# A two-layer matmul kernel on one core: which PSUM banks its products take, and in which order

## The chip, the core and the metric

The kernel runs on one core of a Trainium2 chip. The time is device microseconds of one execution: three runs of the kernel before took 566.67, 566.69 and 568.35 us, the median is 566.69. The profiled execution is a fourth.

The engines are named as in the profile: PE (TensorE, the matmuls), DVE (VectorE), ACT (ScalarE), POOL (GpSimd), SP (SyncE, which issues most loads). Results of PE land in PSUM, which has eight banks; a bank holds 128 x 512 fp32 numbers, one product group. Everything else lies in SBUF.

## The reference

A decayed linear attention over 16 heads (2 batches of 8) of 768 positions and 64 features gives 1536 tokens of 512 features. Two layers follow, each 512 to 2048 to 512, the first with ELU between, the second with a leaky rectifier whose slope is a given number per feature:

```python
x = attention(q, k, v, lam)               # 1536 x 512, causal, decay lam per head
h = x @ w_in;   g = where(h > 0, h, exp(minimum(h, 0)) - 1);       x = g @ w_out
h = x @ w2_in;  g = maximum(h, 0) + alpha * minimum(h, 0);         y = g @ w2_out
```

All is fp32.

## The kernel before

**Precision.** Each fp32 operand is split into a high and a low part in fp32r, and a product is three matmuls: high by high, high by low, low by high. The names end in `h` and `l` (`x0h`, `x0l`, `wah`, `wal`, `wdh`, `wdl`, `wsh`, `wsl`, `qb1h`, ...). The low part of anything is a subtraction by `sub` (L347), which may run on DVE or POOL; the high part is a copy or cast by `copy` (L339, L341) on ACT or DVE. The weights come in by DMA (`raw`), and ACT (L373) and DVE (L375, L378, L381) turn their bits into `wt` before the split.

**Attention** (to about 46 us): twelve blocks of 128 tokens, each with scores (L487), the decay mask on DVE (L492), the state (L531) and the outputs (L556, L562). `run_up` (L474) are matmuls of a constant tile ahead of the first block: three before `lam` is spread (L630), six behind.

**The layers.** The tokens are three chunks of 512: t = 0, 1, 2. Each layer has NU = 8 steps j of 256 hidden features. The way *up* of chunk 0 is `plain` (L707 on): two products of four times three matmuls of 128 x 512, in two groups of six, the result in one bank. Chunks 1 and 2 share one scheme (`seven`, L744 on): seven products of six matmuls instead of eight, on sums of weights (`ws`) and of tokens (`qT1`, `qT2`, `qT3`). Its banks are 0, 1 and 2, turned by j. Four of its results in a bank are not yet final when a product ends: `kept` copies a bank to a `step` tile, and `tile` adds a bank and such a copy (L766). In step j = 0 all three chunks go by `plain`.

`finish` (L670) takes a finished sum to `g`: relu on ACT (L675 from PSUM, L680 from SBUF), in layer 0 exp (L686), a combine on DVE (L688 in layer 0, L692 in layer 1), and the split into high and low of a slot `g`. The way *down* (`down`, L785) is one group of six matmuls (L802) for each t and quarter e, in banks 5, 6 and 7, added to `acc` on DVE (L813).

**Order.** PE's order is written out by hand: `merge(up, dn, lead)` gives out `lead` groups of `up`, then one `up` and one `down` in turn. For the other engines a planner (`Plan`) takes operations by due time as engines come free by its own costs; an operation marked shared (both inputs in SBUF) isn't begun while one of the other of DVE and POOL runs. Each engine then runs its list in that order.

Before step j of `seven`, `weights`, `sums` and `weights_down` convert what the next step needs. `combine` makes the sums of tokens between the layers and behind the attention.

Of the kernel before, what the change touches and what calls it, by code (L numbers as in the profile page):

```python
# [12 lines left out]
ALU = mybir.AluOpType  # L13
# [12 lines left out]
NU = NF // 2  # L26
# [186 lines left out]
def attention_two_layers(  # L213
# [57 lines left out]
    def ut(i):  # L271
        return step(i)
# [341 lines left out]
    def begin():  # L614
# [15 lines left out]
        pe(0.3, lambda: nc.tensor.matmul(  # L630
            out=p_[:, 0:H], lhsT=row[:, 0:128], rhs=row[:, 128:128 + H], start=True, stop=True),
           [b_row, b_one], [b_ps[k]])
        run_up(6)
        op({"DVE": 0.17}, lambda e: nc.vector.tensor_copy(lam_sb, p_[:, 0:H]),
           [b_ps[k]], [b_lam])

# [30 lines left out]
    gslot = {}  # L667
# [39 lines left out]
    def plain(l, j, t=0):  # L707
        for q in range(2):
            f = 2 * j + q
            k = 3 + turn("up", 2)  # L710
            s = j % 2
            mms = [(w, x, cc) for w, x in ((0, 0), (0, 1), (1, 0)) for cc in range(NCC)]
            xs = both[t] if t else x0
            if t:
                b_x = [b_quad[f"B{c}{t}", p, o] for p in range(2) for c in (1, 2)
                       for o in range(2)]
            else:
                b_x = [b_x0[p, o] for p in range(2) for o in range(4)]

            for g in range(2):  # L720
                def run(g=g, q=q, k=k, xs=xs):
                    for i in range(6 * g, 6 * g + 6):
                        w, x, cc = mms[i]
                        nc.tensor.matmul(  # L724
                            out=banks[k], lhsT=wa[s][w][:, cc, q * 128:(q + 1) * 128],
                            rhs=xs[x][:, cc, :], start=i == 0, stop=i == 11)
                yield pe(6 * MM, run, b_x + b_wa[s], [b_ps[k]])
            finish(l, f, lambda k=k: banks[k], b_ps[k], (l, j, q, t), True)
# [15 lines left out]
    def seven(l, j):  # L744
        s = j % 2
        for n, (a, b, k, opens, closes) in enumerate(PRODUCTS):
            k = (k + j) % 3

            def run(a=a, b=b, k=k, opens=opens, closes=closes):
                i = 0  # L750
                for w, x in ((0, 0), (0, 1), (1, 0)):
                    for cc in range(2):
                        nc.tensor.matmul(  # L753
                            out=banks[k], lhsT=left(s, a, w)[:, cc, :],
                            rhs=quad(b, x)[:, cc, :], start=bool(opens and i == 0),
                            stop=bool(closes and i == 5), skip_group_check=True)
                        i += 1
            reads = [b_quad[b, p, o] for p in range(2) for o in range(2)]
            reads += b_wa[s] if a[0] == "A" else b_ws
            yield pe(6 * MM, run, reads, [b_ps[k]])  # L760

            def kept(u, k=k):
                copy(lambda: ut(u), lambda: banks[k], [b_ps[k]], [b_ut[u]], 512, True)

            def tile(u, q, t, k=k):
                op({"DVE": vec(512)}, lambda e: nc.vector.tensor_tensor(  # L766
                    out=ut(u), in0=banks[k], in1=ut(u), op=ALU.add),
                   [b_ps[k], b_ut[u]], [b_ut[u]])
                finish(l, 2 * j + q, lambda: ut(u), b_ut[u], (l, j, q, t), False)
            if b == "B11":  # L770
                kept(0)
            elif b == "B21":
                tile(0, 0, 1)
            elif b == "T1":
                kept(1)
            elif b == "T2":
                kept(2)
            elif b == "B22":
                tile(2, 0, 2)
            elif b == "T3":  # L780
                tile(1, 1, 2)
            else:
                finish(l, 2 * j + 1, lambda k=k: banks[k], b_ps[k], (l, j, 1, 1), True)

# [60 lines left out]

    def downs(l, j, ts):
        for t, e in ts:
            yield from down(l, j, t, e, 2 if (l, j, t, e) == (1, NU - 1, 1, 3) else 1)
            if e == 3:
                gfree.extend(gslot[l, j, q, t] for q in range(2))  # L850

    T0 = [(0, e) for e in range(4)]
    T12 = [(t, e) for t in (2, 1) for e in range(4)]
# [2 lines left out]
    def build():  # L856
# [46 lines left out]
        for l in range(2):  # L903
            if l == 0:
                merge(chain(plain(0, 0, 1), plain(0, 0, 0), at_once(second), plain(0, 1),
                            plain(0, 0, 2)), downs(0, 0, T0), 10)
            else:
                merge((), downs(1, 0, T0))
                merge(chain(plain(1, 0, 1), plain(1, 0, 2)), downs(1, 1, T0))
# [3 lines left out]
            for j in range(1, NU - 1):  # L913
                merge(chain(seven(l, j), at_once(weights, l, j + 1), at_once(sums, l, j + 1),
                            plain(l, j + 1)),
                      chain(downs(0, 1, T0) if (l, j) == (0, 1) else (), downs(l, j - 1, T12),
                            at_once(weights_down, l, j + 1),
                            downs(l, j, T0) if j > 1 else ()), 2 * (l == 1 and j == 1))
            j = NU - 1
            merge(seven(l, j), chain(downs(l, j, T0), downs(l, j - 1, T12)))  # L920
            if l == 1:
                merge((), downs(1, j, T12))
                continue
# [71 lines left out]
```

## Time and profile before

| what | value |
|---|---|
| median of three runs | 566.69 us |
| profiled execution | 567.25 us, its span 565.5 us |
| PE busy | 554.6 us (98%) |
| DVE, ACT, POOL busy | 412.8, 293.6, 306.8 us |
| granted clock, mean of the span | 0.997 |

A row of an engine in time gives its start, how long it lasted, the work, how many instructions, and in brackets the idle time before it and what ended it. Rows of PE hold several matmuls; a matmul starts 0.227 us behind the one before it when nothing waits, and lasts longer than that since they overlap. PEclk is the clock that the throttle granted, as a share of full speed.

### The profile page before, as it was taken

Reading aid. Unit: us, or ns where it says so; the run is one execution under the profiler, and the core shown is the slowest. Engines: PE = TensorE matmul, PEld = TensorE weight load, DVE = VectorE, ACT = ScalarE, POOL = GpSimd, SP = SyncE. Lnnn points to the kernel's source line nnn. Section 1 sums busy time; section 2 is a strip of 40 time slices with the busy share of each in tenths; the row PEclk is TensorE's granted clock in tenths of the full one; section 3 lists DMA queues with packets and bytes.
Section 4 is the critical chain, followed back from the end, with each engine's and each line's share of the span. In section 5 each row is a group of like instructions: output and inputs, shape, how many; then the busy total and the mean of one; then the engine's idle time right before and its main releaser. Section 6 shows DMA issues by size and latency. Waiting matters only on the chain.

```text
span 565.5 us, 7443 instructions
## 1 busy us (share of the span) xinstructions
PE 554.6 (98%) x2870; PEld 458.7 (81%) x2870; DVE 412.8 (73%) x532; ACT 293.6 (52%) x462; POOL 306.8 (54%) x207
## 2 busy tenths in 40 slices
PE   9998999999999999999999989999999999999997
PEld 8887878888888888888878868888888888888886
DVE  6898888647576674768984988667877787877464
ACT  2575676856364646455655626746453434434220
POOL 4885534475746647555648843675746473742000
PEclk9999999999999999999999989999999999999999
DMA  8962422031304021222221202041322222000104
GB/s 346 403 259 81 145 74 75 21 129 32 119 0 150 0 77 72 74 76 75 75 84 65 75 1 69 6 149 37 114 75 74 75 74 75 0 2 0 56 20 148
DMA packets 18309, 49.24 MB, mean 87 GB/s; under 512 B 1250, under 2 KB 1506, under 8 KB 18274
## 3 DMA queue, kind: packets, MB, share of 16 engines
q1 hardware_dynamic: 18128, 48.25, 24.4%
q8 instruction: 22, 0.36, 0.3%
q10 hardware_dynamic: 146, 0.52, 0.2%
q14 instruction: 13, 0.11, 0.1%
HBM read 45.62 MB, written 3.15 MB: 86 GB/s over the span
## 4 chain that ended last, share of the span: by engine, by line
PE 81%; DVE 10%; DMA 3%; issue 2%; ACT 2%; SPq 0%; ACTq 0%; DVEq 0%
PE ps L802 41%; PE ps L753 22%; PE ps L724 15%; DVE wt L381 2%; DMA raw<-in_w1o 1%; DVE wt L378 1%; DVE g L347 1%; DMA raw<-in_w1i 1%; DVE wt L375 1%; DVE acc L813 1%; PE ps L487 1%; DMA raw<-in_w2o 1%; PE ps L474 1%; DVE step L688 1%; PE ps L556 1%
## 5 line engine op out<-in xcount | busy, mean ns | idle before, releaser
L813 DVE TENSOR_TENSOR acc<-ps,acc 128x512 f32<-128x512 f32 (+1 forms) x169 | 115.7, 686 | 93.5 <-PE ps L802 92.5
L347 POOL TENSOR_TENSOR g<-step,g 128x512 fp32r<-128x512 f32 x66 | 103.9, 1576 | 92.7 <-ACT g L339 92.6
L802 PE MATMUL ps<-wdh,g 128*128 128x512 f32 (+1 forms) x388 | 119.2, 388 | 1.9 <-DVE g L347 1.9
L802 PE MATMUL ps<-g,wdh 128*128 128x512 f32 x384 | 118.5, 390 | 0.0
L802 PEld LDWEIGHTS ps<-wdh,g 128*128 128x128 f32 x388 | 73.0, 189 | 17.3 <-DVE g L347 2.3
L802 PEld LDWEIGHTS ps<-g,wdh 128*128 128x128 f32 x384 | 72.0, 188 | 15.5 <-DVE g L347 0.3
L339 ACT CAST g<-step 128x512 fp32r<-128x512 f32 x96 | 59.3, 620 | 43.2 <-DVE step L692 29.0
L802 PE MATMUL ps<-g,wdl 128*128 128x512 f32 x192 | 74.8, 390 | 1.1 <-DVE wdl L347 1.1
L802 PE MATMUL ps<-wdl,g 128*128 128x512 f32 (+1 forms) x194 | 75.2, 387 | 0.0
L347 POOL TENSOR_TENSOR wsl<-wt,wsh 128x1024 fp32r<-128x1024 f32 x13 | 33.7, 2590 | 48.7 <-PE ps L802 19.1
L675 ACT ACTIVATE step<-ps 128x512 f32<-128x512 f32 x54 | 32.4, 599 | 41.8 <-PE ps L724 33.7
L680 ACT ACTIVATE step<-step 128x512 f32<-128x512 f32 x42 | 26.5, 632 | 48.6 <-DVE step L766 48.2
L378 DVE SCALAR_TENSOR_TENSOR wt<-raw,wt 128x1024 uint32<-128x1024 uint32 x32 | 49.6, 1556 | 0.2
L347 POOL TENSOR_TENSOR wt<-wt 128x256 f32<-128x256 f32 x50 | 41.2, 841 | 13.0 <-DVE wt L381 12.2
L347 POOL TENSOR_TENSOR wal<-wt,wah 128x1024 fp32r<-128x1024 f32 x12 | 28.9, 2405 | 33.1 <-ACT wah L339 33.1
L339 ACT COPY step<-ps 128x512 f32<-128x512 f32 x42 | 24.7, 589 | 36.4 <-PE ps L753 36.2
L381 DVE SCALAR_TENSOR_TENSOR wt<-raw,wt 128x1024 uint32<-128x1024 uint32 x32 | 43.5, 1363 | 0.0
L802 PEld LDWEIGHTS ps<-g,wdl 128*128 128x128 f32 x192 | 36.0, 188 | 8.9 <-DVE wdl L347 1.5
L802 PEld LDWEIGHTS ps<-wdl,g 128*128 128x128 f32 x194 | 36.6, 189 | 7.5
L373 ACT ACTIVATE wt<-raw 128x1024 f32<-128x1024 f32 x32 | 36.4, 1139 | 7.6 <-DMA raw<-in_w1i 2.5
L766 DVE TENSOR_TENSOR step<-ps,step 128x512 f32<-128x512 f32 x42 | 28.9, 688 | 14.1 <-PE ps L753 14.0
L724 PE MATMUL ps<-x0l,wah 128*128 128x512 f32 x128 | 38.9, 389 | 0.0
(129 smaller groups left out, 1004.5 us busy)
## 6 DMA issues: line engine op xcount, KB each, us to landing
raw<-in_w1i SPq DMA_DIRECT2D x8, 1024.0 KB, 5.5
raw<-in_w1o SPq DMA_DIRECT2D x8, 1024.0 KB, 4.8
raw<-in_w2i SPq DMA_DIRECT2D x8, 1024.0 KB, 5.4
raw<-in_w2o SPq DMA_DIRECT2D x8, 1024.0 KB, 4.9
blk<-in_kqT SPq DMA_DIRECT2D x12, 512.0 KB, 6.9
blk<-in_vk SPq DMA_DIRECT2D x9, 512.0 KB, 6.9
out<-acc SPq DMA_DIRECT2D x11, 256.0 KB, 2.0
blk<-in_vk ACTq DMA_DIRECT2D x1, 512.0 KB, 6.0
```

The lines of the kernel that those rows point to most:

```text
L339: nc.scalar.copy(dst(), src())
L347: lambda e: on(e).tensor_tensor(out=dst(), in0=a(), in1=b(), op=alu),
L373: op({"ACT": 1.14}, lambda e: nc.scalar.mul(t, upper.bitcast(F32), 2.0 ** -112), [b_r], [b_t])
L378: op({"DVE": vec(1024)}, lambda e: nc.vector.scalar_tensor_tensor(out=tu, in0=lower, scalar=29, in1=tu, op0=ALU.logical_shift_right, op1=A ...
L381: op({"DVE": vec(1024)}, lambda e: nc.vector.scalar_tensor_tensor(out=tu, in0=upper, scalar=0x80000000, in1=tu, op0=ALU.bitwise_and, op1=A ...
L675: op({"ACT": act(512, True)}, lambda e: nc.scalar.activation(rt(i), h(), AF.Relu, scale=-1.0), [b_h], [b_r])
L680: nc.scalar.activation(rt(i), h(), AF.Relu, scale=-1.0)
L724: nc.tensor.matmul(out=banks[k], lhsT=wa[s][w][:, cc, q * 128:(q + 1) * 128], rhs=xs[x][:, cc, :], start=i == 0, stop=i == 11)
L753: nc.tensor.matmul(out=banks[k], lhsT=left(s, a, w)[:, cc, :], rhs=quad(b, x)[:, cc, :], start=bool(opens and i == 0), stop=bool(closes an ...
L766: op({"DVE": vec(512)}, lambda e: nc.vector.tensor_tensor(out=ut(u), in0=banks[k], in1=ut(u), op=ALU.add), [b_ps[k], b_ut[u]], [b_ut[u]])
L802: nc.tensor.matmul(out=p_, lhsT=lhs, rhs=rhs, start=i == 0, stop=i == 5)
L813: op({"DVE": vec(w)}, lambda _, a=a, p_=p_: nc.vector.tensor_tensor(out=a(), in0=p_, in1=a(), op=ALU.add), [b_ps[k], *b_a], b_a)
```

## The change

Four places.

- The second `run_up` has three matmuls instead of six.
- In steps j = 0 and 1 of a layer `plain` takes the banks 3, 4, 0, 1, 2 in turn, instead of 3 and 4. From j = 2 on it takes 3 and 4 as before.
- The sums of `tile` are written to a bank of PSUM instead of the `step` tile: to the product's own bank, for T3 to bank (1 + j) % 3. `finish` reads them there: its relu is L675 instead of L680, and its combine has one operand in PSUM and isn't marked shared.
- Leads: 12 instead of 10 at the start of layer 0; 4 instead of 2 at (layer 1, j = 1); 2 instead of 0 at the last `seven` of each layer. `gfree`, the list of free slots of `g`, gets its slots back one step earlier in the construction.

```diff
-        run_up(6)
+        run_up(3)
...
-            k = 3 + turn("up", 2)
+            k = (3 + turn(("first", l), 5)) % 5 if j < 2 else 3 + turn("up", 2)
...
-            def tile(u, q, t, k=k):
+            def tile(u, q, t, k=k, to=None):
+                to = k if to is None else to
                 op({"DVE": vec(512)}, lambda e: nc.vector.tensor_tensor(
-                    out=ut(u), in0=banks[k], in1=ut(u), op=ALU.add),
-                   [b_ps[k], b_ut[u]], [b_ut[u]])
-                finish(l, 2 * j + q, lambda: ut(u), b_ut[u], (l, j, q, t), False)
+                    out=banks[to], in0=banks[k], in1=ut(u), op=ALU.add),
+                   [b_ps[k], b_ut[u]], [b_ps[to]])
+                finish(l, 2 * j + q, lambda: banks[to], b_ps[to], (l, j, q, t), True)
...
-                tile(1, 1, 2)
+                tile(1, 1, 2, to=(1 + j) % 3)
...
-            yield from down(l, j, t, e, 2 if (l, j, t, e) == (1, NU - 1, 1, 3) else 1)
-            if e == 3:
-                gfree.extend(gslot[l, j, q, t] for q in range(2))
+            parts = 2 if (l, j, t, e) == (1, NU - 1, 1, 3) else 1
+            for c, x in enumerate(down(l, j, t, e, parts)):
+                if e == 3 and c == parts - 1:
+                    gfree.extend(gslot[l, j, q, t] for q in range(2))
+                yield x
...
-                            plain(0, 0, 2)), downs(0, 0, T0), 10)
+                            plain(0, 0, 2)), downs(0, 0, T0), 12)
...
-                            downs(l, j, T0) if j > 1 else ()), 2 * (l == 1 and j == 1))
+                            downs(l, j, T0) if j > 1 else ()), 4 * (l == 1 and j == 1))
...
-            merge(seven(l, j), chain(downs(l, j, T0), downs(l, j - 1, T12)))
+            merge(seven(l, j), chain(downs(l, j, T0), downs(l, j - 1, T12)), 2)
```

Since the planner works with the new needs, its lists move too. The names in the pieces that follow: `g_689` and the like are slots of `g` (numbered anew in each kernel), `wt<-wt` is a sum of weights for `ws`, `wal`, `wdl` and `wsl` are low parts of weights.

DVE behind the attention, before. The last L575, which writes `x0l`, the input of chunk 0's products, stands right ahead of the first row; the `g` of the last row is the one that the first down group reads second:

```order
L381 SCALAR_TENSOR_TENSOR wt<-raw,wt 128x1024
L378 SCALAR_TENSOR_TENSOR wt<-raw,wt 128x1024
L688 SCALAR_TENSOR_TENSOR step<-step,ps 128x512
L347 TENSOR_TENSOR wal<-wt,wah 128x1024
L688 SCALAR_TENSOR_TENSOR step<-step,ps 128x512
L381 SCALAR_TENSOR_TENSOR wt<-raw,wt 128x1024
L347 TENSOR_TENSOR g_689<-step,g_689 128x512
L688 SCALAR_TENSOR_TENSOR step<-step,ps 128x512
L347 TENSOR_TENSOR wdl<-wt,wdh 128x1024
L688 SCALAR_TENSOR_TENSOR step<-step,ps 128x512
L347 TENSOR_TENSOR wt<-wt 128x256
L347 TENSOR_TENSOR g_733<-step,g_733 128x512
```

And now, from the same L381 to the `g` that the first down group reads second:

```order
L381 SCALAR_TENSOR_TENSOR wt<-raw,wt 128x1024
L688 SCALAR_TENSOR_TENSOR step<-step,ps 128x512
L378 SCALAR_TENSOR_TENSOR wt<-raw,wt 128x1024
L347 TENSOR_TENSOR wal<-wt,wah 128x1024
L347 TENSOR_TENSOR g_673<-step,g_673 128x512
L381 SCALAR_TENSOR_TENSOR wt<-raw,wt 128x1024
L688 SCALAR_TENSOR_TENSOR step<-step,ps 128x512 x2
L347 TENSOR_TENSOR g_717<-step,g_717 128x512
L688 SCALAR_TENSOR_TENSOR step<-step,ps 128x512
L347 TENSOR_TENSOR g_706<-step,g_706 128x512
L347 TENSOR_TENSOR wt<-wt 128x256
L347 TENSOR_TENSOR g_737<-step,g_737 128x512
```

The first L688 stands ahead of an L378 instead of behind it, `wdl` has left DVE's list here, and two slots of `g` (`g_717`, `g_706`) stand in it where `wdl` stood and after.

DVE at the last two sums of a round in layer 0 (step j = 4), before. The second L766 is the sum of T3, on which the last product waits:

```order
L813 TENSOR_TENSOR acc_72<-ps,acc_72 128x512
L766 TENSOR_TENSOR step<-ps,step 128x512
L813 TENSOR_TENSOR acc_71<-ps,acc_71 128x512
L375 TENSOR_SCALAR wt<-wt 128x1024
L766 TENSOR_TENSOR step<-ps,step 128x512
L688 SCALAR_TENSOR_TENSOR step<-step 128x512
```

And now:

```order
L814 TENSOR_TENSOR acc_72<-ps,acc_72 128x512
L375 TENSOR_SCALAR wt<-wt 128x1024
L378 SCALAR_TENSOR_TENSOR wt<-raw,wt 128x1024
L814 TENSOR_TENSOR acc_72<-ps,acc_72 128x512
L381 SCALAR_TENSOR_TENSOR wt<-raw,wt 128x1024
L767 TENSOR_TENSOR ps<-ps,step 128x512
L814 TENSOR_TENSOR acc_71<-ps,acc_71 128x512
L767 TENSOR_TENSOR ps<-ps,step 128x512
L688 SCALAR_TENSOR_TENSOR step<-step,ps 128x512
```

The conversion L375 that stood between the two sums now stands ahead of both, and so do L378 and L381.

DVE in layer 1, at the weights of step j = 1, before. The `g` at the end is read by a down group:

```order
L381 SCALAR_TENSOR_TENSOR wt<-raw,wt 128x1024
L813 TENSOR_TENSOR acc_71<-ps,acc_71 128x512
L692 SCALAR_TENSOR_TENSOR step<-step,beta,ps 128x512
L347 TENSOR_TENSOR wdl<-wt,wdh 128x1024
L347 TENSOR_TENSOR qb1l<-acc_71,qb1h 128x512
L347 TENSOR_TENSOR g_803<-step,g_803 128x512
```

And now:

```order
L381 SCALAR_TENSOR_TENSOR wt<-raw,wt 128x1024
L814 TENSOR_TENSOR acc_71<-ps,acc_71 128x512
L692 SCALAR_TENSOR_TENSOR step<-step,beta,ps 128x512
L814 TENSOR_TENSOR acc_72<-ps,acc_72 128x512
L347 TENSOR_TENSOR qb1l<-acc_71,qb1h 128x512
L692 SCALAR_TENSOR_TENSOR step<-step,beta,ps 128x512
L814 TENSOR_TENSOR acc_71<-ps,acc_71 128x512
L347 TENSOR_TENSOR wdl<-wt,wdh 128x1024
L347 TENSOR_TENSOR qb1l<-acc_71,qb1h 128x512
L347 TENSOR_TENSOR g_782<-step,g_782 128x512
```

L381, the end of the conversion, and `wdl`, `qb1l` and `g` keep their order; between L381 and `wdl` there are now three L814 (the renumbered L813), one `qb1l` and two L692.

## Rows read from the trace of the kernel before

**Rows 1.** Waits of PE: for what, us in total, times, longest

```profile
PE ps L724 <- DVE step L688: 2.1, 1, 2.1
PE ps L802 <- DVE g L347: 1.9, 1, 1.9
PE ps L802 <- DVE wdl L347: 1.1, 1, 1.1
```

**Rows 2.** PE in time, 50 to 332: start, us, work, idle before

```profile
52.57 1.07 PE L724 MATMUL ps<-qb1l,wah 128*128 128x512 f32 x4
53.48 1.07 PE L724 MATMUL ps<-qb1h,wal 128*128 128x512 f32 x4
56.68 1.20 PE L724 MATMUL ps<-x0h,wah 128*128 128x512 f32 x4 [2.13 <-DVE step L688]
...
82.03 0.50 PE L802 MATMUL ps<-g,wdl 128*128 128x512 f32 x1 [1.05 <-DVE wdl L347]
...
190.80 0.73 PE L753 MATMUL ps<-qb2h,wah 128*128 128x512 f32 x2
...
192.29 0.61 PE L802 MATMUL ps<-g,wdh 128*128 128x512 f32 x2
...
286.12 0.73 PE L753 MATMUL ps<-qb2h,wah 128*128 128x512 f32 x2 [0.65 <-DVE step L766]
...
327.35 0.50 PE L802 MATMUL ps<-wdh,g 128*128 128x512 f32 x1 [1.93 <-DVE g L347]
```

**Rows 3.** Windows: stretch, length, busy us by engine, PEclk, DMA share

```profile
2.00:36.00 34.00, 33.09 (x464) 29.25 (x463) 29.08 (x56) 17.00 (x40) 23.76 (x21) 1.00 1.02 400
...
328.00:332.00 4.00, 4.00 (x12) 3.14 (x11) 3.97 (x4) 1.31 (x2) 1.53 (x1) 0.57 0.00 0
```

**Rows 4.** PE in time, in the attention part

```profile
3.15 2.93 PE L474 MATMUL ps<-warm 128*128 128x128 f32 x12
6.01 2.60 PE L487 MATMUL ps<-blk 64*128 64x128 f32 x32
...
44.78 1.09 PE L556 MATMUL ps<-smqp,blk 128*64 128x128 f32 x16
```

**Rows 5.** Tile blk, loads issued before 1.3 us, and their landing

```profile
L331 SPq DMA_DIRECT2D blk<-in_kqT x2: 381/400/419, 0.7 to 1.2; - x2
...
DMA to landing us min/median/max: 3.3/5.4/6.0
```

**Rows 6.** DVE in time, eight places of the span

```profile
7.75 1.29 DVE L492 TENSOR_TENSOR smqp<-ps,dmst 128x512 f32<-128x512 f32 x2 [1.58 <-PE ps L487]
...
43.98 0.69 DVE L492 TENSOR_TENSOR smqp<-ps,dmst 128x512 f32<-128x512 f32 x1
...
55.95 0.68 DVE L688 SCALAR_TENSOR_TENSOR step<-step,ps 128x512 f32<-128x512 f32 x1
...
59.92 1.78 DVE L347 TENSOR_TENSOR g<-step,g 128x512 fp32r<-128x512 f32 x1
...
77.29 0.68 DVE L347 TENSOR_TENSOR g<-step,g 128x512 fp32r<-128x512 f32 x1
...
189.45 0.69 DVE L375 TENSOR_SCALAR wt<-wt 128x1024 uint32<-128x1024 uint32 x1 [0.49 <-ACT wt L373]
190.06 0.68 DVE L766 TENSOR_TENSOR step<-ps,step 128x512 f32<-128x512 f32 x1
...
324.45 2.85 DVE L347 TENSOR_TENSOR g<-step,g 128x512 fp32r<-128x512 f32 x1
```

**Rows 7.** ACT in time, ahead of the last attention blocks

```profile
36.74 1.18 ACT L373 ACTIVATE wt<-raw 128x1024 f32<-128x1024 f32 x1 [2.39 <-DMA raw<-in_w1o]
```

**Rows 8.** Groups by form, DVE: busy us, mean ns, idle before

```profile
L688 DVE SCALAR_TENSOR_TENSOR step<-step,ps 128x512 f32<-128x512 f32 x27 | 18.3, 679 | 4.1 <-ACT step L686 4.0
...
L688 DVE SCALAR_TENSOR_TENSOR step<-step 128x512 f32<-128x512 f32 x21 | 15.2, 724 | 2.0 <-ACT step L686 1.9
```

**Rows 9.** POOL in time, at E

```profile
320.59 3.39 POOL L347 TENSOR_TENSOR wsl<-wt,wsh 128x1024 fp32r<-128x1024 f32 x1
```


## The prediction

> **What bounds the kernel now.** I read PE's waits first [rows 1]: one of 2.1 us for DVE's L688, one of 1.9 for a `g`, one of 1.1 for a `wdl`. With 0.65 for an L766 [rows 2] they are 5.8 us of a span of 565.5, and beside them only short waits stand in the list: PE computes nearly all the time. No edit takes a large product away, so the change can only move these waits and what follows them. All of them are waits for DVE. The second view is PE in order of time [rows 2], which gives the waits their places: B (56.68), C (82.03), D (286.12), E (327.35). The third is the granted clock: 0.57 as the mean of the four us behind E [rows 3], so that part of it runs at the lower level, 1.2 GHz instead of 2.4. The work lost is 4 × 0.43 = 1.7 us, and E costs 1.9 + 1.7 = 3.6 us. Behind B, a longer wait, PE's next four matmuls take 1.20 us, near the 1.07 of undisturbed ones: full speed.
>
> **Start: three run-ups fewer.** A run-up is two rows of the trace, and 12 rows take 2.93 us [rows 4]: three save 1.47, if the input of the scores (L487) is there. The first load is issued at 0.7 and lands 3.3 later, at 4.0 [rows 5]; the scores could start at 4.6 instead of 6.01. L492 on DVE waits 1.58 for them at 7.75 [rows 6], so up to 1.4 us could be passed on. But at 36.74 ACT waits 2.39 us for the load of w1o [rows 7], which a faster PE can't bring sooner: the DMA engines' share is 1.02 from 2 to 36 us [rows 3], full. Behind it stands DVE's L492 of 43.98, which ends at 44.67 [rows 6]; PE's L556, which reads it, starts at 44.78 [rows 4] and shows no wait. PE arrives there just in time now, and would wait for what it had saved. I take 0; the ends are −1.4, and +0.3 (if the scores' own input is late after all).
>
> **B: five banks.** PE's third plain product waits 2.13 us [rows 2] because bank 3 is read by DVE's L688 only at 55.95 [rows 6], behind weight conversions. With five banks the third and fourth products take banks that nobody holds; their last input (L575) stands three operations ahead of that L688 on DVE, so it is there. The restart costs 1.20 − 1.07 = 0.13, and 0.2 more for the matmul in flight when PE stopped. B is worth −2.4.
>
> **What is late next: the first down group.** By the new lead PE meets it two groups later in its list, and 2.4 us earlier at each place. A group is six matmuls of (53.48 − 52.57) / 4 = 0.227 us [rows 2], so 1.36; the two add 2.7, and the group starts at the same time as before, about 66.6. It needs the second `g` 0.7 later. DVE makes that `g`; in its list three conversions, four L688, a `wal` and four other `g` or slices stand ahead. An operation of DVE with two inputs in SBUF that meets one of POOL takes longer: a `g` of 1.78 at 59.92, of 0.68 at 77.29 [rows 6]. Laying out the new order with such meetings, the `g` comes at 68.0 to 68.8, a new wait of 0.7 to 1.5; without meetings there is none; with one more there are 2.2. I take +1.0.
>
> **C.** The wait for `wdl` is 1.05 [rows 2], with its restart 1.3. On DVE `wsl`, L381 and `qT2l` stand ahead of `wdl` in the new order, as `wsl` and L381 did; I get its end at 80.3 to 80.8, where PE wants it at 79.0 to 79.5. The wait stays: 0, ends −1.3 and +1.3. B, first down and C: −1.4 together; ends −3.7 (no wait left) and +1.1.
>
> **Sums kept in PSUM.** 42 sums are written to PSUM, and 42 relus and 42 combines read it. No row shows a sum written to PSUM. The nearest is L688, which takes 679 ns with a PSUM operand and 724 without [rows 8]: −0.045 an operation. Beside PE, which waits for neither engine in this stretch but for T4 (below), I cost it at 0; without that cover it is 42 × 0.045 = −1.9, and as much on the other side. A bank is now held until the combine: sum, relu, exp, combine, four operations of some 0.68 = 2.7 us behind the product. The next product into it comes two groups later, with downs between them 4 us. In layer 1 five leading groups have no down between them, 2.7 us: the tightest place, at most +0.5.
>
> T4, the last product of a round, waits for T3's sum. From 190.80 to the next group it takes 1.49 instead of 1.36 [rows 2], and so in five rounds of layer 0. Here the sum of 190.06 started behind an L375 that had itself waited 0.49 for ACT [rows 6]. In the new order a conversion still stands right ahead of it in two of the five rounds: 3 × 0.13 = −0.4, ends 0 and −0.7.
>
> **D.** The last round of layer 0 waits 0.65 for the same sum [rows 2], behind an `x0l` on DVE. All four `x0l` are now POOL's, and lead 2 puts more downs behind the products. −0.5 in all with the restart, ends −0.8 and +0.5.
>
> **E.** DVE's `g` takes 2.85 us at 324.45 [rows 6], since it meets POOL's `wsl` (320.59, 3.39) and its neighbours [rows 9]. In the new order `wdl`, `qb1l`, `g` follow one another on DVE as before, POOL's list keeps `acc`, `wsl`, `qT1l` there, and `wdl` can't start before PE's last read of the old weights and ACT's cast behind it, which the change doesn't move. With meetings the `g` comes at 327.1 to 327.7, where PE wants it at 325.3. I take 0; ends −3.6 (no wait) and +1.3 (one more meeting).
>
> The Trainium skill speaks to both ends of E. "SBUF — State Buffer", Who interferes with whom, says that the engine which issues first holds the shared port and the other blocks for the whole instruction, so issue order decides. The meetings in rows 6 and 9 agree that both suffer; by that rule a `wdl` issued just ahead of POOL's `acc` would come out alone, E would fall to a wait of 0.9, and the total to that of rival 1. "TensorE: Matmul & The Clock Gate", What's actually happening, says that the activity window runs free of the kernel's start; by it, half clock behind a wait is a matter of when it falls. The trace agrees as far as it goes (none behind 2.13 us, some behind 1.93), and a moved E could lose its 1.7 us or a new wait gain them.
>
> **Sum.** Start 0, B, first down and C −1.4, PSUM 0, T4 −0.4, D −0.5, E 0: −2.3, and with the small gain in DVE's operations −2.4. The profiled execution took 567.25 (span 565.5 and 1.75 around it), so 564.85; the median of the runs, 566.69, is 0.56 under it: 564.3.
>
> **Rivals.**
> 1. E shortens too, its half clock included or not. For it: all is shifted by a microsecond there, and the conversions of w2o stand earlier on DVE. Against: the gate of `wdl` stands. A further −1.7 to −3.6: 560.7 to 562.6.
> 2. B's gain is given back whole at the first down (wait 2.2), D and T4 gain half: −0.2 −0.4 = −0.6, so 566.1. For it: what DVE has to do ahead of that `g` is as much in both orders. It holds, too, if the sums in PSUM do nothing at all.
> 3. Slower: the wait at the first down is long enough to be followed by half clock as at E. PE loses 2.2 + 1.7 there, and `wdl` at C, with `qT2l` ahead of it, 1.3 more: −2.4 + 5.2 = +2.8, 569.5. It decides if the second `g` is later than about 69.2, a wait like E's. Against: one wait of three above 1 us was followed by it.
> 4. All goes: −2.4 − 1.3 (C) − 1.4 (start) − 0.5 − 0.8 − 3.6 = −10.0, and no new wait: 556.7. That needs no meeting of DVE and POOL anywhere; the rows speak against.
>
> **Chances.** The forecast (562.8 to 565.6 by itself) 0.47, rival 1 0.18, rival 2 0.19, rival 3 0.10, rival 4 0.06. A measurement of this kernel can tell 0.3%, 1.7 us, from no change: faster is under 565.0, slower over 568.4. Faster: 0.40 of the forecast and rivals 1 and 4, 0.64. Same: 0.07 of the forecast, rival 2 and 0.01 of rival 3, 0.27. Slower: 0.09. The range leaves out rivals 3 and 4 and the far end of nothing else: 560.2 to 567.4.
>
> **What would show it.** In the changed kernel the third plain product should follow the second without a wait; a wait of about 1 us for a DVE `g` should stand at the first down group and one for `wdl` at 79 to 80; T4 should take 1.36 in rounds 4 to 6; a wait of about 2 us for `g` should stand near 322 to 325; and PE should wait before 45 us for what it saved at 5. No wait at the first down makes B worth its 2.4 in full; a wait of a seven product for L688 or L692 would show the PSUM term wrong; no wait for `g` in layer 1 would show E's.

## The result, and the profile after

Four runs of the changed kernel took 561.05 to 561.54 us, median 561.32; the kernel before, beside them, 566.85. The ratio is 0.9896, 95% interval [0.9879, 0.9914]: 5.5 us faster, where 2.4 were forecast. The sign was right, the time lies inside the range, the size was missed by more than a factor of two.

Where the time went is read from PE's list, which holds the same work in nearly the same order in both kernels. Each line compares the start of one instruction at the same point of it:

| up to | before | after | gained in the stretch | forecast |
|---|---|---|---|---|
| first weight product (L724) | 48.83 | 48.83 | 0 | 0 |
| second product of the first round of seven | 83.06 | 80.84 | 2.22 | 1.4 |
| first product of the last round, layer 0 | 268.75 | 265.82 | 0.71 | 0.4 |
| first down group (L802) of layer 1 | 317.56 | 313.42 | 1.21 | 0.5 |
| second plain product behind E | 332.27 | 326.25 | 1.88 | 0 |
| first product of round 2, layer 1 | 369.00 | 363.13 | -0.15 | 0 |
| last matmul | 562.07 | 556.20 | 0 | 0 |

PE of the changed kernel in order of time (start, duration, work, idle before), the places of [rows 2, 4]:

```profile
4.73 3.49 PE L487 MATMUL ps<-blk 64*128 64x128 f32 x32
8.76 0.69 PE L531 MATMUL ps<-blk,kdqs 128*64 128x64 f32 x16 [0.54 <-POOL kdqs L504]
...
44.78 1.09 PE L556 MATMUL ps<-smqp,blk 128*64 128x128 f32 x16
...
54.38 1.07 PE L724 MATMUL ps<-x0h,wah 128*128 128x512 f32 x4
...
68.23 0.50 PE L803 MATMUL ps<-g,wdh 128*128 128x512 f32 x1 [0.54 <-DVE g L347]
...
79.80 0.50 PE L803 MATMUL ps<-g,wdl 128*128 128x512 f32 x1 [0.53 <-DVE wdl L347]
...
80.84 0.62 PE L753 MATMUL ps<-qb1h,wah 128*128 128x512 f32 x2
...
188.30 0.62 PE L753 MATMUL ps<-qb2h,wah 128*128 128x512 f32 x2
...
189.66 0.62 PE L803 MATMUL ps<-g,wdh 128*128 128x512 f32 x2
...
322.94 0.50 PE L803 MATMUL ps<-wdh,g 128*128 128x512 f32 x1 [1.65 <-DVE g L347]
...
326.25 1.07 PE L724 MATMUL ps<-qb1h,wah 128*128 128x512 f32 x4
```

Of the kernel before, the rows that stand against 8.76, 80.84 and 326.25:

```profile
8.54 0.69 PE L531 MATMUL ps<-blk,kdqs 128*64 128x64 f32 x16
...
83.06 0.63 PE L753 MATMUL ps<-qb1h,wah 128*128 128x512 f32 x2
...
332.27 1.08 PE L724 MATMUL ps<-qb1h,wah 128*128 128x512 f32 x4
```

The scores start 1.28 us earlier, and L556 of [rows 4] starts at 44.78 again: the run-ups are given back. That is done by 8.76, where PE, with a first block of scores of 3.49 instead of 2.60 and a wait of 0.54 for POOL's `kdqs`, is 0.22 later than before. The third plain product follows at 54.38 without a wait. A wait of 0.54 stands at the first down group and one of 0.53 for `wdl`. T4 takes 189.66 - 188.30 = 1.36. D's wait is gone. E is still there, 1.65 for 1.93. The windows behind it (stretch, length, busy time of PE, PEld, DVE, ACT, POOL, granted clock, DMA share, GB/s) answer to [rows 3]:

```profile
324.00:328.00 4.00, 4.00 (x19) 3.33 (x18) 2.89 (x4) 2.85 (x4) 2.33 (x1) 1.00 0.00 0
328.00:332.00 4.00, 4.00 (x19) 3.30 (x19) 3.73 (x5) 0.84 (x2) 0.10 (x1) 1.00 0.02 4
```

The clock stays at 1.00 where it was 0.57, the mean of a stretch most of which was at half clock (0.50, 1.2 GHz instead of 2.4). That is the one stretch with a gain of 1.9 where the forecast had none. DVE and POOL at E, after:

```profile
314.84 2.46 DVE L347 TENSOR_TENSOR wdl<-wt,wdh 128x1024 fp32r<-128x1024 f32 x1 [0.53 <-ACT wdh L339]
317.23 2.88 DVE L347 TENSOR_TENSOR qb1l<-acc,qb1h 128x512 fp32r<-128x512 f32 x1
320.03 2.86 DVE L347 TENSOR_TENSOR g<-step,g 128x512 fp32r<-128x512 f32 x1
```

```profile
316.19 3.37 POOL L347 TENSOR_TENSOR wsl<-wt,wsh 128x1024 fp32r<-128x1024 f32 x1
319.52 2.82 POOL L347 TENSOR_TENSOR qT1l<-acc,qT1h 128x1024 fp32r<-128x1024 f32 x1
```

As in [rows 6, 9], `g` takes four times its 0.68 us. Groups by form on DVE (busy, mean ns, idle before), for [rows 8]:

```profile
L688 DVE SCALAR_TENSOR_TENSOR step<-step,ps 128x512 f32<-128x512 f32 x48 | 32.6, 681 | 4.1 <-ACT step L686 3.6
L767 DVE TENSOR_TENSOR ps<-ps,step 128x512 f32<-128x512 f32 x42 | 29.3, 698 | 19.0 <-PE ps L753 18.0 <-ACT x0h L339 0.7
```

The sums of the kernel before:

```profile
L766 DVE TENSOR_TENSOR step<-ps,step 128x512 f32<-128x512 f32 x42 | 28.9, 688 | 14.1 <-PE ps L753 14.0
```

A sum written to PSUM takes 698 ns, 10 more than one written to SBUF took.

Executions of one and the same kernel come at levels about 1.6 us apart, and each level has its own mean clock. The kernel before, 63 executions on the four chips of the experiments:

| mean granted clock | executions | time, median |
|---|---|---|
| 1.000 | 16 | 565.3 |
| 0.996 to 0.997 | 27 | 567.0 |
| 0.993 to 0.994 | 20 | 568.5 |

The profiled execution (567.25, 0.997) is of the middle level. The four runs of the changed kernel are all at 0.999 or 1.000. Level against level the change is worth 565.3 - 561.3 = 4.0 us; the other 1.5 is half clock that the kernel before has in most executions and the changed one in none. On each of the four chips the kernel before has its first level between 565.1 and 565.5 (medians), so versions that ran on different chips compare to about 0.4 us.

### The profile page after: what moved, and what is told of

Same layout as the page of the kernel before. It is cut to its first block, busy times and chain, and to the rows that moved or that the text cites. A ratio compares the mean times of both kernels' runs of the same rounds, so it can differ in the third digit from the quotient of the medians.

```text
span 559.6 us, 7427 instructions
## 1 busy us (share of the span) xinstructions
PE 551.4 (99%) x2864; PEld 457.4 (82%) x2864; DVE 397.6 (71%) x523; ACT 292.4 (52%) x461; POOL 312.6 (56%) x217
## 4 chain that ended last, share of the span: by engine, by line
PE 86%; DVE 6%; DMA 4%; ACT 2%; issue 1%; SPq 0%; ACTq 0%; DVEq 0%
PE ps L803 44%; PE ps L753 24%; PE ps L724 15%; DMA raw<-in_w1i 2%; DMA raw<-in_w1o 2%; DVE g L347 1%; PE ps L487 1%; DVE wt L381 1%; DVE wt L347 1%; PE ps L556 1%; DVE wdl L347 1%; DVE smqp L492 1%; PE ps L562 1%; PE ps L474 1%; DVE qb1l L347 1%
## 5 line engine op out<-in xcount | busy, mean ns | idle before, releaser
L814 DVE TENSOR_TENSOR acc<-ps,acc 128x512 f32<-128x512 f32 (+1 forms) x169 | 116.0, 687 | 97.4 <-PE ps L803 96.7
L347 POOL TENSOR_TENSOR g<-step,g 128x512 fp32r<-128x512 f32 x73 | 106.4, 1462 | 80.9 <-ACT g L339 80.7
L675 ACT ACTIVATE step<-ps 128x512 f32<-128x512 f32 x96 | 57.4, 598 | 95.2 <-DVE ps L767 51.4
L347 POOL TENSOR_TENSOR wsl<-wt,wsh 128x1024 fp32r<-128x1024 f32 x12 | 31.8, 2650 | 54.7 <-ACT wsh L339 33.5
L692 DVE SCALAR_TENSOR_TENSOR step<-step,beta,ps 128x512 f32<-128x512 f32 x48 | 35.7, 743 | 18.5 <-ACT step L675 18.5
L347 POOL TENSOR_TENSOR wal<-wt,wah 128x1024 fp32r<-128x1024 f32 x14 | 34.5, 2465 | 23.4 <-ACT wah L339 23.3
L381 DVE SCALAR_TENSOR_TENSOR wt<-raw,wt 128x1024 uint32<-128x1024 uint32 x32 | 44.4, 1389 | 0.0
L347 POOL TENSOR_TENSOR wdl<-wt,wdh 128x1024 fp32r<-128x1024 f32 x12 | 32.2, 2683 | 20.1 <-ACT wdh L339 19.9
L767 DVE TENSOR_TENSOR ps<-ps,step 128x512 f32<-128x512 f32 x42 | 29.3, 698 | 19.0 <-PE ps L753 18.0
L378 DVE SCALAR_TENSOR_TENSOR wt<-raw,wt 128x1024 uint32<-128x1024 uint32 x32 | 41.7, 1308 | 0.1
L347 POOL TENSOR_TENSOR wt<-wt 128x256 f32<-128x256 f32 x51 | 38.7, 774 | 5.0 <-DVE wt L381 3.9
```

Source lines behind the costliest of these rows:

```text
L347: lambda e: on(e).tensor_tensor(out=dst(), in0=a(), in1=b(), op=alu),
L378: op({"DVE": vec(1024)}, lambda e: nc.vector.scalar_tensor_tensor(out=tu, in0=lower, scalar=29, in1=tu, op0=ALU.logical_shift_right, op1=A ...
L381: op({"DVE": vec(1024)}, lambda e: nc.vector.scalar_tensor_tensor(out=tu, in0=upper, scalar=0x80000000, in1=tu, op0=ALU.bitwise_and, op1=A ...
L675: op({"ACT": act(512, True)}, lambda e: nc.scalar.activation(rt(i), h(), AF.Relu, scale=-1.0), [b_h], [b_r])
L692: op({"DVE": vec(512) + 0.06}, lambda e: nc.vector.scalar_tensor_tensor(out=rt(i), in0=rt(i), scalar=beta[:, f:f + 1], in1=h(), op0=ALU.mu ...
L767: op({"DVE": vec(512)}, lambda e: nc.vector.tensor_tensor(out=banks[to], in0=banks[k], in1=ut(u), op=ALU.add), [b_ps[k], b_ut[u]], [b_ps[to]])
```

## The experiments

**Undoing one part of the change at a time.** The run-ups:

```diff
-        run_up(3)
+        run_up(6)
```

> The changed kernel with all six run-ups again. My theory: PE waits for the same load (w1o) and DVE's L492 by 45 us in any case, so the first weight product (L724) starts at 48.83 as in both kernels, and the time is that of the changed kernel, 561.3, within 0.4. Rival (the run-ups saved are passed on): 561.3 + 1.4 = 562.7.

Measured: 561.25 (561.21 to 561.44), the time of the changed kernel. The run-ups are worth nothing either way, as forecast. The reason given, that PE waits for the load of w1o and for DVE by 45 us, is not what the rows show: the difference is gone at 8.76 us already, where L531 starts in both.

Banks 3 and 4 only:

```diff
-            k = (3 + turn(("first", l), 5)) % 5 if j < 2 else 3 + turn("up", 2)
+            k = 3 + turn("up", 2)
```

> The changed kernel, but plain products take banks 3 and 4 throughout, as before. My theory: the wait at 54.5 for L688 of 1 to 2.3 us returns, and the first down group then comes late enough to have its second g in time (0.7 returned), so the stretch to the first seven-product round loses 1.5 to 2: 562.8 to 563.3, and the rest of the trace is as in the changed kernel, without half clock. Rival A (DVE's list moves so that L688 comes at 55.0): the wait is under 0.7, time 561.3 to 561.8. Rival B (everything behind it shifts, and half clock at the wait for g in layer 1 returns): 564.5 to 565.

Measured: 563.04 (562.93 to 563.26), 1.7 more. PE, in order of time:

```profile
54.99 1.20 PE L724 MATMUL ps<-x0h,wah 128*128 128x512 f32 x4 [0.65 <-DVE step L688]
...
61.80 1.21 PE L724 MATMUL ps<-x0h,wah 128*128 128x512 f32 x4 [0.89 <-DVE step L688]
...
68.11 1.20 PE L724 MATMUL ps<-qb2h,wah 128*128 128x512 f32 x4 [0.53 <-DVE step L688]
```

One wait of 2.1 has become three of 0.5 to 0.9, for the same L688, and no half clock follows any. The theory holds in the time and in the sum of the waits, not in their form: it had one wait.

Sums in SBUF (`tile` and its T3 call as before):

```diff
-                    out=banks[to], in0=banks[k], in1=ut(u), op=ALU.add),
-                   [b_ps[k], b_ut[u]], [b_ps[to]])
-                finish(l, 2 * j + q, lambda: banks[to], b_ps[to], (l, j, q, t), True)
+                    out=ut(u), in0=banks[k], in1=ut(u), op=ALU.add),
+                   [b_ps[k], b_ut[u]], [b_ut[u]])
+                finish(l, 2 * j + q, lambda: ut(u), b_ut[u], (l, j, q, t), False)
```

> The changed kernel, but the tile sums go to SBUF and finish reads them there, as before. My theory: the product behind the T3 sum takes 1.50 again in five or six rounds of layer 0 (+0.7), the last round of layer 0 gets part of its 1.2 back, and nothing else moves: 562.0 to 563.0. Rival A (the leads alone made these gains): 561.3. Rival B (the planner's list moves so that the wait for g in layer 1 is followed by half clock): 1.7 more, 563.7 to 564.7.

Measured: 561.00 (560.83 to 561.04). The theory is wrong, and rival A is nearer by its time: T4 still takes 1.36 in all rounds of layer 0. With banks and leads, the sums in PSUM have nothing left to do.

Old leads (10, 2, 0):

```diff
-                            plain(0, 0, 2)), downs(0, 0, T0), 12)
+                            plain(0, 0, 2)), downs(0, 0, T0), 10)
...
-                            downs(l, j, T0) if j > 1 else ()), 4 * (l == 1 and j == 1))
+                            downs(l, j, T0) if j > 1 else ()), 2 * (l == 1 and j == 1))
...
-            merge(seven(l, j), chain(downs(l, j, T0), downs(l, j - 1, T12)), 2)
+            merge(seven(l, j), chain(downs(l, j, T0), downs(l, j - 1, T12)))
```

> The changed kernel with the leads 10, 2 and 0 of before. My theory: five banks take away the wait at 54.5 in any case, but the first down group comes two groups earlier and waits 2 to 3 us longer for its second g, so B's 2.3 is given back there; the last round of layer 0 loses the 0.5 to 0.8 of its T4: 563.3 to 564.5. Rival (the leads matter for nothing): 561.3, with the wait for g at the first down group below 0.6.

Measured: 563.58, at levels: 561.9 and 562.2 (clock 1.000), 563.5 to 563.8 (0.996 to 0.997), 564.8 (0.993).

```profile
68.15 0.50 PE L803 MATMUL ps<-g,wdh 128*128 128x512 f32 x1 [2.53 <-DVE g L347]
...
342.89 0.50 PE L803 MATMUL ps<-wdh,g 128*128 128x512 f32 x1 [0.67 <-DVE g L347]
```

At clock 1.000 the old leads cost 0.7 us (562.06 for 561.32); the rest of the 2.3 is half clock. The early part is as expected: B is given back in a wait of 2.53. The late part was not expected: E is gone, 0.67 at another `g` is all that is left, and from the last round of layer 0 to round 2 of layer 1 PE needs 96.2 us for 97.3 with the new leads.

**One part alone, on the kernel before.** Banks (the edit of the two banks, the other way round):

> The kernel before with the five banks alone. The runs of the kernel before come at three levels, 565.5, 567.1 and 568.6, with mean clocks of 1.000, 0.997 and 0.993; I read them as none, one or two stretches of half clock, one behind the 1.9 us wait for g in layer 1 (E), one behind the 2.1 us wait for bank 3 (B). Theory: without B's wait but with E's, only two levels are left, about 1.6 apart; B's gain is partly given back at the first down group, as with the old leads in the changed kernel (2.5 us wait there): lowest level 563.5 to 565.0. If a wait of over 1.9 us stands at the first down group, the third level comes back. Rival: the stretches have nothing to do with these waits; three levels stay whatever the waits are.

Measured: 566.46. Four executions at 564.5 to 564.9 (1.000), three at 566.4 to 566.5, one at 568.0 (0.994), four at 568.8 to 569.0 (0.991). In the profiled one, 569.03, two waits and the windows behind them:

```profile
67.92 0.79 PE L802 MATMUL ps<-g,wdh 128*128 128x512 f32 x1 [2.53 <-DVE g L347]
```

```profile
66.00:74.00 8.00, 6.08 (x15) 4.78 (x16) 7.01 (x7) 4.22 (x7) 5.86 (x4) 0.57 0.01 2
74.00:82.00 8.00, 8.00 (x37) 6.61 (x36) 6.11 (x7) 5.84 (x10) 0.00 (x0) 1.00 0.40 131
329.00:333.00 4.00, 3.83 (x10) 3.00 (x11) 4.00 (x4) 0.52 (x2) 2.35 (x1) 0.61 0.00 0
```

B's wait has gone to the first down group, there are two waits near or over 2 us again (2.53, and 1.91 at E), and half clock behind both. The reading of the levels holds only in part. Two such waits bring half clock again, as expected, but in four clocks and not three: behind the 2.53 it stays for nearly the whole of 66 to 74, about twice as long as behind E. So a level tells how much half clock there was, not how many waits had it behind them. Alone the banks gain 0.6 us on the first level, 564.7 for 565.3.

Sums in PSUM alone:

> The kernel before with the tile sums in PSUM alone. Theory (from the changed kernel with sums in SBUF, which took 561.0, not more than 561.3): the sums in PSUM are worth nothing by themselves; lowest level 565.0 to 566.0, and the waits at B and E stay. Rival: they take the 0.14 per round off the product behind T3's sum, and D: lowest level 563.8 to 564.8.

Measured: 562.31 and 562.37 (1.000), 563.64 to 563.99 (0.997): the rival, and beyond it. T4 takes 1.36 in all rounds, and E is gone:

```profile
344.42 0.50 PE L803 MATMUL ps<-wdh,g 128*128 128x512 f32 x1 [0.67 <-DVE g L347]
```

Only B (1.96 here) is left to be followed by half clock, and there are two levels. The profiled execution (563.64) has the half clock at that place:

```profile
56.30 1.94 PE L724 MATMUL ps<-x0h,wah 128*128 128x512 f32 x4 [1.96 <-DVE step L688]
```

```profile
56.00:60.00 4.00, 3.70 (x9) 2.94 (x10) 3.92 (x5) 1.86 (x4) 3.03 (x2) 0.57 0.75 250
```

So sums in PSUM alone give 2.9 us (two executions at 1.000), three quarters of the whole, and given the other parts they give nothing. What both have in common is DVE's list: where T4 loses 0.14, an L375 stands between the last two sums (in five rounds before, in five with the banks alone and in five with the leads alone); where it doesn't, that L375 has moved or has its input in time. This is read from the orders; no run moves that L375 alone.

Leads alone:

> The kernel before with the leads 12, 4 and 2 alone (and the slots of g returned a step earlier). Theory: B's wait for bank 3 stays in part (0.6 to 2.1, spread over several products, as in the changed kernel with two banks), no wait at the first down group, T4 takes 1.36 and D goes: lowest level 562.8 to 564.0, without half clock where no wait is over 1.9. Rival: without five banks the leads only move the waits: 565.5.

Measured: 565.30 and 565.38 (1.000), the others 567.0 to 568.3: the rival, nothing gained. The theory is wrong: three waits for L688 are left in the early part (2.2 together), T4 still takes 1.49 to 1.50 in six rounds of layer 0, and what PE has gained up to E, E loses again:

```profile
327.10 0.80 PE L802 MATMUL ps<-wdh,g 128*128 128x512 f32 x1 [2.53 <-DVE g L347]
```

**The start's new lead without the others.**

```diff
-                            downs(l, j, T0) if j > 1 else ()), 4 * (l == 1 and j == 1))
+                            downs(l, j, T0) if j > 1 else ()), 2 * (l == 1 and j == 1))
...
-            merge(seven(l, j), chain(downs(l, j, T0), downs(l, j - 1, T12)), 2)
+            merge(seven(l, j), chain(downs(l, j, T0), downs(l, j - 1, T12)))
```

> The changed kernel with lead 12 kept at the start, but the leads of layer 1 step 1 and of the last seven-product rounds as before (2 and 0). With the old leads everywhere the stretch from the last round of layer 0 to step 2 of layer 1 took 96.2 us against 97.3 in the changed kernel, and the stretch before the first seven-product round 1.5 more. Theory: the two add up independently, 561.3 - 1.1 = 560.2, with the wait for g in layer 1 at 0.7 instead of 1.65. Rival: the planner's lists of the late part hang on the early part as well; 561.0 to 562.0.

Measured: 559.99 (559.86 to 560.02), ratio 0.9874 [0.985, 0.9897] to the kernel before: 1.3 us better than the changed kernel and within 0.2 of what the theory gave. DVE's `g` at E meets nobody there and takes 0.68:

```profile
319.77 0.68 DVE L347 TENSOR_TENSOR g<-step,g 128x512 fp32r<-128x512 f32 x1
```

The same with sums in SBUF (both edits from above):

> Five banks, lead 12 at the start, the other leads as before, tile sums in SBUF as before. With the leads of the changed kernel the sums in SBUF took 561.0 instead of 561.3. Theory: with the other leads as before, the sums decide the planner's list at the last rounds of layer 0 and at layer 1 step 1, as in the kernel before with the sums alone (its lowest level was 2.9 below that of the kernel before, and its wait for g in layer 1 0.67 instead of 1.93): with sums in SBUF the wait of 1.9 is back, and D: 561.5 to 563, with half clock in some executions. Rival: the late part hangs on the lead and banks alone: 559.7 to 560.0.

Measured: 559.87 (559.79 to 560.39). My theory fell, the rival held: E does not come back without the sums in PSUM; a wait of 0.34 at 268.32 is new.

Lead 14 and lead 11 at the start, the late leads as before:

> The best version so far (changed kernel, leads 2 and 0 in the late part as before, 559.99) with lead 14 instead of 12 at the start. Theory: the wait for the second g at the first down group (0.5, 0.7 with its restart) goes, but PE then comes 0.7 earlier to the wdl that DVE ends at 79.7, so the wait of 0.53 there grows by as much: 559.8 to 560.2. Rival: the two are independent: 559.3.

Measured: 566.76 (566.18 to 567.44), 6.8 us slower than with 12, and all ten executions at a clock of 0.993 to 0.994.

```profile
82.40 1.19 PE L803 MATMUL ps<-g,wdh 128*128 128x512 f32 x2 [4.50 <-DVE wdh L341]
```

```profile
82.00:86.00 4.00, 3.15 (x7) 2.08 (x8) 3.79 (x6) 0.18 (x1) 0.00 (x0) 0.50 0.63 254
86.00:90.00 4.00, 4.00 (x14) 3.19 (x13) 1.42 (x3) 1.60 (x4) 2.53 (x2) 0.71 0.00 0
```

Theory and rival both missed it: the planner's list brings the cast `wdh` on DVE only at 81.09, and PE waits 4.5 us at C. In the profiled execution the clock is 0.50 behind it and 0.71 as the mean of the next four us, as long as behind the 2.53 of the banks alone; the other nine were not profiled, and their mean clock is the same.

> The same with lead 11. Theory: the first down group comes 1.36 us earlier than with lead 12, its second g when DVE gets to it, so the wait grows from 0.5 to 1.5 to 1.9 and is not made up: 560.8 to 561.4, no half clock. Rival: the planner takes the g earlier, as its due time is earlier: 560.0.

Measured: 560.18 (560.11, 560.13, 560.23; one of 561.73 at 0.997). The wait at the first down group is 1.88, as expected:

```profile
68.02 0.50 PE L803 MATMUL ps<-g,wdh 128*128 128x512 f32 x1 [1.88 <-DVE g L347]
```

But it is made up: C's wait for `wdl` is gone, since PE gets there later. The theory missed the time for that reason, and half clock in one execution of four; the rival met the time, not the reason.

**What E's wait is.** The first attempt gave the planner a dependency of `wsl` on the `g`:

```diff
...
+            sub(lambda: fs[1], lambda: y, lambda: fs[0].bitcast(F32),
+                [b_y, b_ws[0], b_g[gslot[1, 1, 1, 0]]], [b_ws[1]], 1024)
...
```

> The changed kernel with one more dependency: the low part wsl of layer 1 step 1 is made only after the g that PE waits for at 322.9. On POOL wsl and qT1l change places; DVE's list stays. Theory: that wait of 1.65 is the price of DVE's wdl, qb1l and g (2.46, 2.88 and 2.86 us) meeting POOL. Now POOL has to pause when g runs, g takes 0.7 instead of 2.86, and the wait and its restart go: 561.3 - 1.8 = 559.5, if wsl isn't late for the third product of that round. Rival A: g starts late for another reason (ACT's casts, PE's last read); wait stays over 1.2, 561.0 to 561.5. Rival B: the late wsl makes a new wait in front of a product with ws: 560.3 to 561.5.

Measured: 561.19 (561.05 to 561.25, and one of 562.46 at clock 1.000 that no profile explains), the wait 1.63. It tested less than was meant. POOL did not pause: `wsl` starts at 319.28, while the `g` ends at 322.65. `qT1l` and `wsl` only changed places:

```profile
315.94 3.38 POOL L347 TENSOR_TENSOR qT1l<-acc,qT1h 128x1024 fp32r<-128x1024 f32 x1
319.28 2.82 POOL L347 TENSOR_TENSOR wsl<-wt,wsh 128x1024 fp32r<-128x1024 f32 x1
```

The second attempt lets POOL read four columns of the `g` first, so that it has to wait:

```diff
...
+            sub(lambda: fill[:, 0:4], lambda: gt(s)[:, 1, 0:4].bitcast(F32),
+                lambda: gt(s)[:, 1, 4:8].bitcast(F32), [b_g[s]], [b_fill], 4, ("POOL",))
+            sub(lambda: fs[1], lambda: y, lambda: fs[0].bitcast(F32),
+                [b_y, b_ws[0], b_fill], [b_ws[1]], 1024, ("POOL",))
...
```

> The changed kernel; POOL gets one tiny operation that reads the g that PE waits for at 322.9, ahead of wsl, so that POOL stands still from the end of its acc (about 316.2) until this g is made. DVE keeps the order wdl, qb1l, g there. Theory (the wait is the price of meeting POOL): wdl still meets acc, qb1l and g take 0.68 to 0.7 each instead of 2.88 and 2.86, g is ready by 319, the wait of 1.65 goes: 561.3 - 1.8 = 559.5, up to 560.3 if the qT1l that the planner then gives to DVE comes late for the next round. Rival (g waits for something else): the wait stays over 1, 560.8 or more.

Measured: 559.02 (558.92 to 559.10), ratio 0.9868 [0.9842, 0.9893], the fastest version here, 2.3 us better than the changed kernel. DVE and POOL at E:

```profile
314.47 2.44 DVE L347 TENSOR_TENSOR wdl<-wt,wdh 128x1024 fp32r<-128x1024 f32 x1 [0.52 <-ACT wdh L339]
316.83 0.68 DVE L347 TENSOR_TENSOR qb1l<-acc,qb1h 128x512 fp32r<-128x512 f32 x1
317.44 0.68 DVE L347 TENSOR_TENSOR g<-step,g 128x512 fp32r<-128x512 f32 x1
```

```profile
313.42 2.41 POOL L347 TENSOR_TENSOR acc<-acc 128x1024 f32<-128x1024 f32 x1
318.19 0.58 POOL L347 TENSOR_TENSOR fill<-g 128x4 f32<-128x4 f32 x1 [2.36 <-DVE g L347]
318.89 2.41 POOL L347 TENSOR_TENSOR acc<-acc,acc 128x1024 f32<-128x1024 f32 x1
```

`wdl` still meets `acc`; `qb1l` and `g` meet nobody, take 0.68 each for 2.88 and 2.86, and PE shows no wait at E. Between the two profiles E gives 1.95 (the wait and its restart) and T4 of layer 1's round 1, which takes 1.49 in the changed kernel and 1.36 here, about 0.15. The rest of what goes beyond the expected 1.8 stands ahead of the layers: the first L724 starts at 48.49 for 48.83, where the edit changes nothing and other profiles lie between. So E's wait is the price of those meetings, shown with the order of `wdl`, `qb1l`, `g` on DVE unchanged.

**What half clock hangs on.** Half of `wdl` is made a second time, between `qb1l` and `g`:

```diff
+        if (l, j) == (1, 1):
+            sub(lambda: fd[1]()[:, 0:512], lambda: t2[:, 0:512],
+                lambda: fd[0]()[:, 0:512].bitcast(F32), [b_t2, b_wd[s][0], b_wd[s][1]], [b_wd[s][1]], 512,
+                ("DVE",))
```

> The changed kernel with half of wdl of layer 1 step 1 made a second time on DVE, between qb1l and the g that PE waits for. Only the length of this one wait changes, from 1.65 to 2.0 to 4.2. Theory (half clock follows waits of nearly 2 us and more in a part of the executions, and waits of 1.65 in none): executions fall into two levels, one at 561.3 plus what the wait grew, clock 1.000, and one 1.6 to 1.8 above it, clock 0.996 to 0.997; if the wait is over 4, nearly all are at the second. Rival (it was a matter of other things that the change moved): all at the first, clock 0.999 to 1.000.

Measured: three executions at 561.8 to 562.1 (1.000), three at 563.5 to 563.6 (0.997).

```profile
322.86 0.50 PE L807 MATMUL ps<-wdl,g 128*128 128x512 f32 x1 [2.08 <-DVE wdl L347]
```

The same place, with a wait of 2.08 for 1.65, goes with half clock in three of six executions, and 0 of 4 had it in the changed kernel. The profiled execution is one of the three without it, so where it fell in the others is inferred from this wait being the only one over 1.5 us. All kernels, by the waits over 1.5 us in their profiles and the clock of each execution:

| kernel | waits over 1.5 us | executions | with a clock under 0.999 |
|---|---|---|---|
| changed kernel, run-ups 6, two banks, sums in SBUF, lead 12 (both), `wsl`, POOL held | 1.65 at most, or none | 42 | 0 |
| lead 11 | 1.88 | 4 | 1 |
| sums alone | 1.96 | 5 | 3 |
| `wdl` made again | 2.08 | 6 | 3 |
| leads alone | 2.53 | 10 | 8 |
| old leads | 2.53 | 6 | 4 |
| before | 2.13, 1.93 | 63 | 47 |
| banks alone | 2.53, 1.91 | 12 | 8 |
| lead 14 | 4.50 | 10 | 10 |

Where a profile has half clock, it begins in one of these waits or right behind it. Leads alone and old leads have one such wait, and each has one execution at 0.993 (568.29, 564.79), as much half clock as behind two waits of the kernel before: a wait can be followed by a longer stretch, as in the profiles of the banks alone and of lead 14.

## Why the prediction was wrong, point by point

- **Start.** Right in the sum, 0, shown by the run-ups put back, and wrong in the way: the saved time was to be lost to the load of w1o and DVE's L492 before 45 us. It is lost at the first block: L531 waits 0.54 for POOL's `kdqs` and starts at 8.76 for 8.54. From 15.29 on PE is where it was, so the bound that the prediction named was never reached, and the 0 owes something to luck.
- **B.** Right in mechanism and size: the third product comes 2.30 earlier, 2.4 with its restart.
- **First down.** The wait came where it was forecast, but it is 0.54, 0.7 with its restart, instead of +1.0: the `g` was made at 68.2, the early end of what I had laid out.
- **C.** "The wait stays: 0" was wrong in size: 0.53 for 1.05, since `wdl` ends at 79.75, earlier than the 80.3 that I had. First down and C are the 0.8 missing in that stretch.
- **T4.** Mis-sized, -0.4 for -0.7: all five rounds were freed, also the two where a conversion stands ahead of the sum. In the first of them the L375 starts at 123.83 without its wait for ACT, and the sum at 124.58, in time.
- **D.** Mis-sized, -0.5 for -1.2: I had priced the wait of 0.65, not T4's own 0.14 there, nor 0.2 at the second product of that round.
- **PSUM.** "Cost it at 0" was right for the operations (698 ns for 688) and too narrow as a view: the part that I took to be worth nothing by its durations is, alone, worth 2.9 us; that it acts by DVE's list is read from the orders, not tested.
- **E.** The step that failed: "I take 0; ends -3.6 (no wait) and +1.3". The wait stayed, as said (1.65), but 1.88 us went. The working priced half clock as part of E, 1.7 us that follow if the wait stays. It is a second quantity: it follows waits of 1.88 and more in a part of the executions, and none of 1.63 to 1.65 (26 executions). In the profiled executions a wait shorter by 0.28 saved 0.28 and the 1.6 behind it. This is rival 1 by its time, 560.7 to 562.6, and by the half of its mechanism that it had a chance for, 0.18.
- **Against which time.** The forecast started from one execution with one stretch of half clock and a median of the same level. From 565.3, where the kernel before has none, the change gains 4.0, and the forecast's 2.4 would have been short by the sizes above alone.

One kernel with one wait of 1.9 to 2.5 us shows half clock in some executions and not in others. The rule of the Trainium skill that the activity window runs free of the kernel's start ("TensorE: Matmul & The Clock Gate", What's actually happening) agrees with that. The prediction named it, and did not carry it into the sum as a chance. With POOL held, `g` takes 0.68, with POOL running 2.86: the Trainium skill's rule that a DVE instruction with two SBUF inputs contends with GpSimd ("SBUF — State Buffer", Who interferes with whom) agrees as well.

Of the miss, by these steps, E is 1.9 of the 3.5 us that the profiles show beyond the forecast; first down and C are 0.8, T4 and D 1.0; 0.15 went the other way.

What is not settled: `wdl` starts behind POOL's `acc` in the changed kernel and with POOL held (314.47 behind 313.42), so the case that the prediction named, a `wdl` issued ahead of it, did not occur there; the 1.93 and 2.13 of the kernel before were not told apart by how often each is followed by half clock; and why the planner's list moves as it does with each single part was read from the orders, not tested.

## What to carry to other kernels

Price a PE wait near 2 us with its chance of half clock behind it, as counted on the kernel at hand, and look at the clock of every execution of the kernel before, not of the profiled one: its levels here lie 3.2 us apart, more than most parts of the change are worth. Where a planner sets the order, parts of a change don't add up (0.6, 2.9 and 0.0 alone, 4.0 together, and taking out the 2.9 costs nothing): measure a part by its removal and alone, and read what it does to the lists. Before moving work to POOL beside a chain of DVE operations with two SBUF inputs that PE waits for, see what runs on POOL then; POOL's pause of 2.4 us went with a gain of 2.3 us here.

## What the runs showed of the hardware

At E a DVE subtraction of 128x512 with both inputs in SBUF takes 0.68 us alone and 2.86 to 2.88 beside POOL's 128x1024 subtractions, which take 2.8 to 3.4 then and 2.41 alone. Kernels with a PE wait of 4.5 us had a mean clock of 0.993 to 0.994 in ten of ten executions (0.50 behind the wait in the one profiled), kernels with waits of 1.88 to 2.53 a clock under 0.999 in a part of theirs, and of 42 executions of kernels without a wait over 1.65, 26 of them with one of 1.63 to 1.65, none did. Each 0.003 of the mean clock goes with 0.9 to 1.8 us. A sum of PSUM and SBUF takes the same on DVE whether it is written to PSUM (698 ns) or SBUF (688).
